# Start offsets for some 150 tasks and a five-transfer queue rule in the list scheduler of an attention and MLP kernel

## The chip, the cores and the metric

The kernel runs on one core of a Trainium2 chip. The metric is the device time of one execution in microseconds (us); lower is better. A core has five instruction streams that run side by side and wait for each other through semaphores: TensorE (PE: matmuls and transposes; its weight loads are shown as PEld), VectorE (DVE), ScalarE (ACT), GpSimd (POOL) and SyncE (SP, which issues all the DMA transfers here). Each stream is strictly in order: an instruction that waits holds back everything behind it on its engine.

## What is computed

Two attentions over the same q, k and v are added, and the sum goes through a two-layer MLP:

```python
# q, k, v: (8 batches, 8 heads, 576 positions, 64)
q_d = q.reshape(B, H, 144, 4, 64).mean(axis=3)        # k_d, v_d alike
out_up = np.repeat(sm_attn(q_d, k_d, v_d), 4, axis=2) # pooled attention, full softmax
mask = np.abs(pos[:, None] - pos[None, :]) < 4        # local attention: 7 neighbours
out_local = softmax(where(mask, q @ k.T * scale, -1e9)) @ v
x = (out_up + out_local).transpose(0, 2, 1, 3).reshape(4608, 512)
h = x @ w_in                                          # 512 -> 2048
return np.maximum(0.01 * h, h) @ w_out                # 2048 -> 512
```

## The kernel before

**Chunks and passes.** The 4,608 rows of x are cut into 13 chunks of columns (batch 0 is chunks 0 and 1 with 256 and 320 columns; chunk 2 has 256, chunk 3 has 320, the rest 384). TensorE makes a pass over the weights for each chunk: for each of 16 slices f of the hidden layer an up-projection into a bank `hp` (`up_proj`, L872), a leaky ReLU on ACT and DVE (`leaky`, L882 to L885), and a down-projection into four banks `acc0` to `acc3`, one for each slice e of the output (`down_proj`, L912). Each product is three matmuls, of a high and a low part of weights and of x, so 24 matmuls for one f. Chunk 0 is done in two passes (f 0 to 7, then, after the pass of chunk 1, f 8 to 15). At the end of a pass `store` copies each `acc` on ACT to a buffer `o` (L957; two buffers in the first pass), and `send` writes it out by DMA. Until the copy is done the bank can't take the next pass.

**Weights.** `convert(f, k)` loads one slice of `w_in` (k=0) or `w_out` (k=1), 512 KB of raw 64-bit numbers, into a staging buffer, and makes the two parts of it with a cast on ACT (L330), a merge on DVE (L332), a second cast on ACT or DVE (L346, L343) and a subtraction on POOL (L348). The first slices stage in buffers that the attention uses later (`k`, `v`, `prod`, `up`); once the work of batch 0 is done, its pool of tiles is given back (`swap`), and the last slices stage in tiles named `w` that lie there.

**Attention.** For batch 0 everything is on TensorE (`pooled`, L451 to L490, and `banded`, L626 to L694). For batches 1 to 7 the pooled part is `pair` (L503 to L581), and the local part runs on POOL and DVE: `scores` (products on POOL at L735, sums on DVE at L743, softmax) and `values` (products on POOL at L794, sums on DVE at L801 into `xloc`). `landing` then turns `xloc` over on TensorE (L831), adds the pooled part (DVE L838) and writes the two parts of x (ACT L844, DVE L846). The first up-projection of a pass waits until all landings of its chunk are done.

**What sets the order.** Every piece of work is a task (a Python generator) with a rank. `Order.run` is a list scheduler that runs while the kernel is built: it keeps a clock for each engine, asks each task for its next operation, and emits the one that can start first by its own costs, the lower rank first where two tie. What it emits stands in that order on the engines for good. The ranks come from `od.spawn(rank, ...)`; for instance a conversion has 20 + 2f + k, the up- and down-projections come last with 4999 and 5000. DMA transfers have one clock too, `wire`, the time when all transfers issued so far would be through at 270 GB/s; a transfer may not be issued while `wire` lies more than 6 us ahead:

```python
if size:
    start = max(start, self.wire - 6.0)
...
if size:
    self.wire = max(self.wire, start + 1.2) + size / RATE
    done = self.wire + 0.8
```

These clocks exist only while the order is made. The chip sees the order and the semaphores, and SP issues a transfer as soon as its buffers are free.

Of the kernel before, what the change touches and what calls it, by code (L numbers as in the profile page):

```python
# [79 lines left out]
OMAX = max(XMAX)  # L80
COST = {"ACT": (0.13, 0.00083), "DVE": (0.08, 0.00104), "POOL": (0.25, 0.00217)}
HOP = 0.4
RATE = 270e3
SAFE = 0.4
POLICIES = [0]
SCARCE, HURRY = ("pt",), 1000
GIVE = {"POOL": 0.3, "DVE": 0.3, "ACT": 0.3}

# [27 lines left out]
class Slot:  # L116
    def __init__(self, order, tag, index, t, task):
        self.order, self.tag, self.index, self.t, self.task = order, tag, index, t, task
        self.push = HURRY if tag in SCARCE else 0
        task[0] -= self.push  # L120
# [6 lines left out]
class Order:  # L127
# [7 lines left out]
    def __init__(self, bufs, policy):  # L135
        self.policy = policy
        self.bufs = bufs
        self.released = {tag: [] for tag in bufs}
        self.engine = dict.fromkeys(("PE", "DVE", "ACT", "POOL", "SP"), 0.0)
        self.wire = 0.0  # L140
        self.port = {"DVE": 0.0, "POOL": 0.0}
        self.events = {}
        self.tasks = []
        self.count = 0
        self.log = []

    def spawn(self, rank, gen):
        self.count += 1
        task = [rank, self.count, gen, None]
        self.tasks.append(task)  # L150
        self.resume(task, None)

# [28 lines left out]
    def run(self):  # L181
        while self.tasks:
            for task in sorted((t for t in self.tasks if t[3][0] != "op"), key=lambda t: t[:2]):
                got = self.grant(task)
                if got is not None:
                    self.resume(task, got)
                    break
            else:
                best = None
                ahead = {eng: [] for eng in GIVE}  # L190
                for task in self.tasks:
                    if task[3][0] == "op" and task[3][1] in GIVE:
                        ahead[task[3][1]].append((max(self.engine[task[3][1]], task[3][3]), task[0]))
                for task in self.tasks:
                    if task[3][0] == "op":
                        _, eng, dur, ready, size, port = task[3]
                        start = max(self.engine[eng], ready)
                        if port:
                            start = max(start, self.port["DVE" if eng == "POOL" else "POOL"])
                        if size:  # L200
                            start = max(start, self.wire - 6.0)
                        if eng in GIVE:
                            late = start + GIVE[eng] * dur
                            start = min((at + 0.01 for at, rank in ahead[eng] if rank < task[0] and start < at < late), default=start)
                        key = (start, task[0], task[1])
                        if best is None or key < best[0]:
                            best = key, task
                assert best is not None, [t[3] for t in self.tasks]
                (start, _, _), task = best
                _, eng, dur, ready, size, port = task[3]  # L210
                free = self.engine[eng]
                self.engine[eng] = start + dur
                if port:
                    self.port[eng] = start + dur
                if size:
                    self.wire = max(self.wire, start + 1.2) + size / RATE
                    done = self.wire + 0.8
                else:
                    done = start + dur + HOP
                self.log.append((start, eng, dur, task[0], start - free, ()))  # L220
                self.resume(task, done)
# [849 lines left out]
```

## Time and profile before

| | |
|---|---|
| median of 3 runs (range) | 934.78 us (931.5 to 936.12) |
| the profiled execution | 935.61 us |
| its span, first to last instruction | 933.8 us |
| mean granted TensorE clock | 0.984 of full speed |
| busy: PE, DVE, ACT, POOL | 910.1, 579.5, 419.8, 568.1 us |
| DMA, mean over the span | 127 GB/s |

The profiled execution lies 0.83 us above the median, and its span 1.81 us below its time, so a span of this kernel and the median differ by 0.98 us. Busy time is that of instructions that ran; idle time of an engine is put down to whatever released it. The granted clock is the share of full speed (2.4 GHz) that TensorE was given, and 0.50 is its other level (1.2 GHz).

### The profile page before, as it was taken

The numbers are of one execution on the slowest core, as the hardware profiler recorded it, in microseconds if no ns is written. First come the engines' busy times: TensorE is split into PE (matmuls) and PEld (weight loads), VectorE is DVE, ScalarE is ACT, GpSimd is POOL, SyncE is SP. The second block draws the span as 40 slices with busy tenths as digits, with TensorE's granted clock in tenths as the row PEclk, the third lists the DMA queues.
The fourth block names the chain that finished last, engine by engine and source line by source line (L and its number), as shares of the span: only waits on it lengthen the run. The fifth ranks groups of instructions, "written<-read, shape, count | busy, mean of one in ns | idle before, by whom it ended". The sixth has DMA issues, their size and how long they took to land.

```text
span 933.8 us, 16676 instructions
## 1 busy us (share of the span) xinstructions
PE 910.1 (97%) x6352; PEld 884.1 (95%) x6352; DVE 579.5 (62%) x941; ACT 419.8 (45%) x1161; POOL 568.1 (61%) x276
## 2 busy tenths in 40 slices
PE   6997999999999999999999999999999999999998
PEld 4787999899999999999999999999999999999998
DVE  4796678878887987876655963953764743311111
ACT  3776547546655545446224544443423423322211
POOL 4555679788889889876966853963974963000000
PEclk7799899999999999999999999999999999999999
DMA  9769565665555554661423541630430410000000
GB/s 243 269 197 315 192 194 153 197 195 145 164 170 162 159 156 113 206 188 56 137 82 106 178 143 29 199 98 26 136 112 26 138 43 26 35 1 1 34 1 35
DMA packets 60977, 118.13 MB, mean 127 GB/s; under 512 B 7440, under 2 KB 26640, under 8 KB 60896
## 3 DMA queue, kind: packets, MB, share of 16 engines
q1 hardware_dynamic: 60896, 117.06, 41.7%
q8 instruction: 50, 0.82, 0.4%
q14 instruction: 31, 0.25, 0.1%
HBM read 107.07 MB, written 9.96 MB: 125 GB/s over the span
## 4 chain that ended last, share of the span: by engine, by line
PE 93%; DVE 2%; DMA 2%; ACT 1%; issue 1%; POOL 1%; SPq 0%; DVEq 0%; POOLq 0%; ACTq 0%
PE acc L912 42%; PE hp L872 42%; PE pt L831 1%; PE pt L533 1%; PE pt L557 1%; PE pt L574 1%; PE acc L451 1%; PE pt L634 1%; DMA w<-in_w_out_dram 1%; DMA vs<-in_vs_dram 1%; POOL w L348 1%; DMA band_sb<-in_band_dram 0%; PE pt L675 0%; PE hp L457 0%; ACT pds L472 0%
## 5 line engine op out<-in xcount | busy, mean ns | idle before, releaser
L794 POOL TENSOR_TENSOR prod<-v,s 128x1344 f32<-128x1344 f32 (+1 forms) x88 | 262.4, 2985 | 84.0 <-DVE xloc L801 78.6
L735 POOL TENSOR_TENSOR prod<-q,k 128x1365 f32<-128x1365 f32 (+1 forms) x88 | 240.1, 2731 | 32.8 <-DVE s L743 20.9
L885 DVE TENSOR_TENSOR gl<-hp,gh 128x384 fp32r<-128x384 f32 (+2 forms) x208 | 108.8, 524 | 243.0 <-ACT hp L883 242.0
L882 ACT ACTIVATE gh<-hp 128x384 fp32r<-128x384 f32 (+2 forms) x208 | 97.5, 469 | 323.6 <-PE acc L912 314.8
L912 PE MATMUL acc<-gh,w 128*128 128x384 f32 (+2 forms) x832 | 217.0, 327 | 0.0
L872 PE MATMUL hp<-xh,w 128*128 128x384 f32 (+2 forms) x832 | 215.9, 327 | 0.6 <-DVE gl L885 0.6
L872 PEld LDWEIGHTS hp<-xh,w 128*128 128x128 f32 x832 | 148.1, 188 | 2.0 <-issue 1.2
L912 PEld LDWEIGHTS acc<-gh,w 128*128 128x128 f32 x832 | 148.3, 188 | 1.3 <-issue 1.0
L912 PE MATMUL acc<-gh,woh 128*128 128x384 f32 (+2 forms) x416 | 138.3, 332 | 5.6 <-ACT o L957 5.5
L872 PE MATMUL hp<-xh,wih 128*128 128x384 f32 (+2 forms) x416 | 140.0, 337 | 0.5 <-DVE gl L885 0.5
L912 PE MATMUL acc<-gh,wol 128*128 128x384 f32 (+2 forms) x416 | 135.7, 326 | 0.5 <-POOL wol L348 0.5
L743 DVE TENSOR_REDUCE s<-prod 128x21 f32<-128x1365 f32 (+1 forms) x88 | 131.4, 1494 | 7.4 <-POOL prod L735 7.3
L912 PE MATMUL acc<-gl,woh 128*128 128x384 f32 (+2 forms) x416 | 135.5, 326 | 0.0
L872 PE MATMUL hp<-xh,wil 128*128 128x384 f32 (+2 forms) x416 | 135.2, 325 | 0.0
L872 PE MATMUL hp<-xl,wih 128*128 128x384 f32 (+2 forms) x416 | 135.2, 325 | 0.0
L912 PE MATMUL acc<-gl,w 128*128 128x384 f32 (+2 forms) x416 | 134.7, 324 | 0.0
L872 PE MATMUL hp<-xl,w 128*128 128x384 f32 (+2 forms) x416 | 134.7, 324 | 0.0
L801 DVE TENSOR_REDUCE xloc<-prod 128x192 f32<-128x1344 f32 (+1 forms) x88 | 130.4, 1481 | 5.3 <-POOL prod L794 5.2
L883 ACT ACTIVATE hp<-hp 128x384 f32<-128x384 f32 (+2 forms) x208 | 96.2, 462 | 0.0
L912 PEld LDWEIGHTS acc<-gh,woh 128*128 128x128 f32 x416 | 78.8, 189 | 8.0 <-ACT o L957 6.0
L872 PEld LDWEIGHTS hp<-xh,wih 128*128 128x128 f32 x416 | 78.5, 189 | 3.2 <-issue 2.0
L912 PEld LDWEIGHTS acc<-gh,wol 128*128 128x128 f32 x416 | 78.7, 189 | 0.7 <-POOL wol L348 0.7
(174 smaller groups left out, 1195.8 us busy)
## 6 DMA issues: line engine op xcount, KB each, us to landing
k<-in_kb_dram SPq DMA_DIRECT2D x76, 292.5 KB, 2.8
v<-in_vb_dram SPq DMA_DIRECT2D x76, 288.0 KB, 2.9
qk<-in_qkt_dram SPq DMA_DIRECT2D x32, 576.0 KB, 7.7
vs<-in_vs_dram SPq DMA_DIRECT2D x56, 144.0 KB, 3.4
q<-in_qb_dram SPq DMA_DIRECT2D x76, 97.5 KB, 1.9
out_dram<-head SPq DMA_DIRECT2D x18, 192.0 KB
out_dram<-o SPq DMA_DIRECT2D x18, 192.0 KB, 2.6
k<-in_kb_dram SPq DMA_DIRECT2D x12, 260.0 KB, 7.6
```

The source lines that it names most:

```text
L348: nc.gpsimd.tensor_tensor(out=lo, in0=tf, in1=hi.bitcast(F32), op=ALU.subtract)
L451: nc.tensor.matmul(sc[rows, qi * SD:(qi + 1) * SD], qk_d[rows, qi * QB:qi * QB + 64], qk_d[rows, SD:2 * SD], start=True, stop=True)
L533: nc.tensor.matmul(scs[p][outs, qi * SD:(qi + 1) * SD], qk_d[i][rows, qi * QB:qi * QB + 64], qk_d[i][rows, SD:2 * SD], start=True, stop=True)
L735: nc.gpsimd.tensor_tensor(out=prv, in0=q[:, :nj].unsqueeze(2).to_broadcast([128, nj, W, DE]), in1=view(half(s_k), 0, [[DE, nj], [DE, W], [ ...
L743: nc.vector.tensor_reduce(out=s[:, p, :nj], in_=prv, axis=AX.X, op=ALU.add)
L794: nc.gpsimd.tensor_tensor(out=prv, in0=view(half(s_v), 0, [[1, nj], [nv, D], [1, W]]), in1=s[:, p, :nj].unsqueeze(2).to_broadcast([128, nj ...
L801: nc.vector.tensor_reduce(out=xl_t[:, :nj, p], in_=prv, axis=AX.X, op=ALU.add)
L872: nc.tensor.matmul(hp[:, :n], wt[:, c], x[:, c], start=k == 0, stop=k == 3 * NC - 1)
L882: nc.scalar.activation(out=gh[:, :n], in_=hp[:, :n], func=AF.Prelu, alpha=0.01)
L883: nc.scalar.activation(out=hp[:, :n], in_=hp[:, :n], func=AF.Prelu, alpha=0.01)
L885: nc.vector.tensor_tensor(out=gl[:, :n], in0=hp[:, :n], in1=gh[:, :n].bitcast(F32), op=ALU.subtract)
L912: nc.tensor.matmul(acc[:, :n], wt[:, es], g[:, :n], start=f == f0 and j == 0, stop=f == f1 - 1 and j == 2)
```

## The change

No operation is added or left out. The scheduler is given another rule for DMA and a table of offsets, and emits another order:

- Instead of the 6 us limit, an operation of SP may not start before the fifth last transfer has landed by the scheduler's clocks (`DEEP = 5`).
- `POLICIES` holds one table, `SHIFTS`, of some 150 numbers by the running number of a task (24 to 224), which `spawn` adds to the task's rank. Most are under 10 in size. They fall on conversions, `pair`, `scores`, `widen` and `values` of the first batches, and on others that are spawned early.

```diff
+DEEP = 5
 RATE = 270e3
 SAFE = 0.4
-POLICIES = [0]
+SHIFTS = {
+    24: 9.7, 27: 5.4, 28: -0.3, 30: 3, 32: 2.8, 33: -0.92, 36: -0.3, 37: -0.52, 38: 1.15, 40: 1.7, 41: 0.95, 42: 8.2, 43: -11.2, 48: -0.3,
...
+}
+POLICIES = [SHIFTS]
...
         self.wire = 0.0
+        self.landed = []
...
-        task = [rank, self.count, gen, None]
+        task = [rank + self.policy.get(self.count, 0), self.count, gen, None]
...
-                        if size:
-                            start = max(start, self.wire - 6.0)
+                        if len(self.landed) >= DEEP and eng == "SP":
+                            start = max(start, self.landed[-DEEP])
...
                     self.wire = max(self.wire, start + 1.2) + size / RATE
+                    self.landed.append(self.wire)
```

All lines behind the table stand 15 lines lower in the changed kernel (L957 is L972 there).

**SP, from the last of the six loads into the given-back tiles.** `w` rows are loads of weights, `up` too; `out_dram<-o` are the first pass's results; `k`, `q`, `vs` and `v` are the first loads for batch 1. Before:

```order
L259 DMA w_0_1013<-in_w_in_dram 128x2048
L259 DMA up<-in_w_out_dram 128x2048
L259 DMA vs<-in_vs_dram 48x768 x2
L259 DMA k<-in_kb_dram 128x520
L259 DMA q<-in_qb_dram 128x130
L259 DMA k<-in_kb_dram 128x520
L259 DMA w_1_1135<-in_w_out_dram 128x2048
L259 DMA out_dram<-o 128x256 x2
```

With the change:

```order
L274 DMA w_0_1039<-in_w_in_dram 128x2048
L274 DMA out_dram<-o 128x256 x2
L274 DMA up<-in_w_out_dram 128x2048
L274 DMA k<-in_kb_dram 128x520
L274 DMA vs<-in_vs_dram 48x768 x2
L274 DMA v<-in_vb_dram 128x512
L274 DMA out_dram<-o 128x256 x2
L274 DMA w_1_1159<-in_w_out_dram 128x2048
```

The first two results go out straight behind the six loads, and the other two ahead of the next load of weights; the six loads stand in one row in both.

**ACT, around the copies of the first pass's results to `o`.** `head<-` rows are the casts of freshly landed weights, `gh` and `hp` rows the leaky ReLU, `acc_693` and `acc_700` (`acc_660` and `acc_666` with the change) the third and the fourth bank. Before, from the copies of the first two banks:

```order
L957 COPY o<-acc_688 128x256
L330 CAST head_76<-w_1_1010 128x512
L882 ACTIVATE gh<-hp 128x320
L883 ACTIVATE hp<-hp 128x320
L346 CAST w_0_1168<-w_0_1009 128x512
L330 CAST head_75<-w_0_1011 128x512
L330 CAST head_76<-w_1_1012 128x512
L346 CAST w_0_1219<-w_0_1011 128x512
L330 CAST head_75<-w_0_1013 128x512
L330 CAST head_76<-w_1_1135 128x512
L957 COPY o<-acc_693 128x256
L957 COPY o<-acc_700 128x256
```

With the change, up to the same copies (those of the first two banks stand five rows ahead of this piece):

```order
L345 CAST head_76<-w_1_1034 128x512
L575 COPY ptd<-pt 128x3x2x48
L897 ACTIVATE gh<-hp 128x320
L898 ACTIVATE hp<-hp 128x320
L345 CAST head_75<-w_0_1035 128x512
L596 COPY outd<-pt 64x144 x4
L897 ACTIVATE gh<-hp 128x320
L898 ACTIVATE hp<-hp 128x320
L972 COPY o<-acc_660 128x256
L972 COPY o<-acc_666 128x256
```

Before, the casts of all six loads and of one load issued after them (`w_1_1135`) stand ahead of the copies of the third and fourth bank; with the change only those of the first two of the six.

**ACT, in the start, from the first cast of weights on.** `pds` is the softmax of heads 4 and 5 (c=2 in `pooled`, with `acc3_229` before and `pt_220` with the change), `su_pd` with `acc0` that of c=3, `su_ptd` and `outd` copies of c=1 to 3, `k_73` and `v_74` the first two loads of weights. Before:

```order
L330 CAST head0_75<-k_73 128x512
L692 CAST xh0_88<-hp_257 128x256
L490 COPY su_ptd_246<-acc1_247 72x3x2x48
L490 COPY su_ptd_246<-pt_297 72x3x2x48
L472 ACTIVATE pds_65,acc3_229<-acc3_229,st_d_255 128x144 x3
L645 ACTIVATE xloc_288<-xloc_288 128x280
L346 CAST wih_0_69<-k_73 128x512
L442 COPY outd_86<-pt_303 128x144
L472 ACTIVATE su_pd_317,acc0_294<-acc0_294,st_d_316 128x144 x3
```

With the change:

```order
L487 ACTIVATE pds_65,pt_220<-pt_220,st_d_242 128x144 x3
L345 CAST head0_75<-k_73 128x512
L707 CAST xh0_88<-acc1_255 128x256
L505 COPY su_ptd_262<-acc2_263 72x3x2x48
L345 CAST head1_76<-v_74 128x512
L505 COPY su_ptd_262<-acc3_315 72x3x2x48
L660 ACTIVATE xloc_291<-xloc_291 128x280
L505 COPY su_ptd_317<-hp_318 72x3x2x48
L505 COPY su_ptd_317<-pt_335 72x3x2x48
L664 ACTIVATE lst_292<-lst_292 128x4
L457 COPY outd_86<-pt_325 128x144
L487 ACTIVATE su_pd_308,acc0_280<-acc0_280,st_d_307 128x144 x3
```

The softmax of c=2 moved ahead of the first cast of weights, the second cast of weights moved up between the copies of c=1, and the softmax of c=3 moved a few places back.

## Rows read from the trace of the kernel before

**Rows 1.** Page, part 1: busy us, share of the span, instructions.
```profile
PE 910.1 (97%) x6352; PEld 884.1 (95%) x6352; DVE 579.5 (62%) x941; ACT 419.8 (45%) x1161; POOL 568.1 (61%) x276
```

**Rows 2.** PE's waits, whole span: us in total, times, longest.
```profile
PE pt L626 <- DMA band_sb<-in_band_dram: 6.1, 1, 6.1
PE acc L912 <- ACT o L957: 5.5, 2, 5.3
...
PE acc L912 <- DVE head L949: 0.2, 1, 0.2
```

**Rows 3.** Windows of the start: length, busy us by engine, PEclk, DMA share, GB/s.
```profile
14.00:26.00 12.00, 12.00 (x87) 8.44 (x85) 5.27 (x14) 5.98 (x21) 5.68 (x7) 0.50 1.02 279
26.00:34.00 8.00, 6.22 (x89) 4.69 (x85) 7.38 (x20) 7.39 (x27) 3.69 (x4) 0.93 0.94 294
34.00:42.00 8.00, 7.65 (x77) 5.71 (x75) 5.20 (x13) 5.54 (x13) 5.33 (x6) 0.50 0.52 172
```

**Rows 4.** Timeline of the start: start, us, instruction, idle before and its releaser.
```profile
23.35 0.77 ACT L330 CAST head<-k 128x512 f16<-128x512 bf16 x1 [1.76 <-DMA k<-in_w_in_dram]
28.03 0.91 POOL L422 TENSOR_TENSOR pds<-pds,st_d 128x432 f32<-128x432 f32 x1 [6.38 <-ACT outd L442]
31.20 0.52 PE L661 MATMUL pt<-id_sb,xloc 128*70 128x128 f32 x3 [1.44 <-DVE xloc L642]
```

**Rows 5.** Chain that ended last, from 84 us: start, us, what.
```profile
84.05 5.24 DMA w<-in_w_out_dram
...
90.00 2.20 DVE w L332
...
92.79 1.40 ACT head L330 x2
94.18 0.23 ACT o L957
...
99.91 3.52 PE hp L872 x24
```

**Rows 6.** Timeline of SP's issues and one DVE sum, same columns as Rows 4.
```profile
72.60 0.33 SPq L259 DMA_DIRECT2D w<-in_w_out_dram  x1
78.39 0.91 SPq L259 DMA_DIRECT2D vs<-in_vs_dram  x2
89.13 0.95 DVE L520 TENSOR_REDUCE v_d<-vs 128x192 f32<-128x768 f32 x1 [2.06 <-DMA vs<-in_vs_dram]
```

**Rows 7.** Windows around PE's long wait, columns as in Rows 3.
```profile
70.00:89.20 19.20, 18.00 (x160) 16.59 (x158) 10.81 (x21) 15.13 (x35) 10.03 (x9) 1.00 0.95 306
89.20:94.50 5.30, 0.04 (x1) 0.04 (x1) 4.60 (x4) 2.27 (x5) 3.98 (x4) 0.70 0.99 360
94.50:98.10 3.60, 3.60 (x14) 3.60 (x15) 0.83 (x3) 0.95 (x3) 1.67 (x1) 0.50 0.97 347
```

**Rows 8.** Timeline of the last landings of chunks 3 and 4, columns as in Rows 4.
```profile
216.63 1.07 DVE L801 TENSOR_REDUCE xloc<-prod 128x128 f32<-128x896 f32 x1
218.91 0.38 PE L831 MATMUL pt<-id_sb,xloc 128*128 128x128 f32 x2
...
281.09 0.55 DVE L846 TENSOR_TENSOR xl<-pt,xh 128x384 fp32r<-128x384 f32 x1
283.05 0.42 PE L872 MATMUL hp<-xh,wih 128*128 128x384 f32 x1
```

**Rows 9.** Window from the long wait to chunk 3, columns as in Rows 3.
```profile
95.00:214.70 119.70, 118.11 (x1016) 114.82 (x1015) 95.36 (x177) 68.99 (x211) 92.47 (x51) 0.99 0.58 180
```

**Rows 10.** POOL's waits, 95 to 140 us, columns as in Rows 2.
```profile
POOL w L348 <- DVE w L343: 7.3, 4, 2.6
POOL w L348 <- ACT w L346: 4.9, 3, 3.6
```

**Rows 11.** ACT's waits, 95 to 140 us, columns as in Rows 2.
```profile
ACT gh L882 <- PE acc L912: 10.0, 9, 2.9
```

**Rows 12.** SP's own waits, whole span, columns as in Rows 2.
```profile
SPq L259 <- ACT o L957: 15.4, 15, 3.6
```

9 rows, old and new, of the table SHIFTS are left out of this document.

## The prediction

> **What bounds the kernel now.** I read the page's busy times first: TensorE is busy 97% of the span [rows 1], so 933.8 - 910.1 = 23.7 us is all the idle time there is, and the change adds and removes no work. A new order can win from two things only: this idle time, and stretches in which TensorE ran at half its clock. So the next view is TensorE's waits [rows 2]. Two of the 14 carry half of the idle time: 6.1 us at the start, for the first data, and 5.3 us for a copy from a bank to `o`. The rest are under 2 us each. Then the windows: from 14 to 26 us and from 34 to 42 us the granted clock was 0.50 [rows 3], and again from 94.5 to 98.1 us, behind the long wait [rows 7]. From there to the end TensorE hardly waits. So the start (to 42 us) and the stretch around 90 us hold what can be won.
>
> **The long wait.** The chain shows what ended it [rows 5]: a load of weights issued at 84.05 landed 5.24 us later, DVE merged it (2.20 us with another), ACT made two casts (1.40 us), and only then came the copy to `o` that frees the bank. The copy itself needed none of this. It stood behind those casts on ACT, which is in order; TensorE was done with the bank long before. DVE had been late too: it held still 2.06 us for a `vs` transfer that was issued at 78.39 and had landed only at 89.13, 10.7 us later [rows 6], because six loads of 512 KB stood in the queue from 72.60 on, with DMA 95 to 99% busy [rows 6, 7].
>
> **The change, part by part.** Base: the profiled span, 933.8 us; the median of the runs is 0.98 us above it.
>
> *The rule of five transfers.* On the chip it costs nothing and limits nothing: it only moves the scheduler's clocks, and SP still has the six loads in one row. What it can do is make the scheduler expect late landings, and place work accordingly.
>
> *The copies on ACT.* They now stand ahead of the casts that held them. What is late next is their target: `o` has two buffers, so the third copy waits until the first result has left, and that transfer now stands right behind the six loads. Six loads and two results are 6 x 0.524 + 2 x 0.131 = 3.41 MB; at the 306 GB/s measured there [rows 7] that is 11.1 us from the first load on, at the 360 GB/s of the next stretch 9.5 us, plus 0.23 us of the copy that the chain shows [rows 5]. Meanwhile TensorE has, by the new order, 12 matmuls of 256 columns and 42 of 320 before it needs that bank. 24 matmuls of 320 columns take 3.52 us, so 0.147 us each [rows 5], and in proportion 0.118 us for 256 columns (an estimate): 6.2 + 1.4 = 7.6 us, and beside them some transposes and products of `pair` that I leave uncosted. So the wait that is left lies between 0 and 11.3 - 7.6 = 3.7 us. I take 1.3, about a third of the bound, since the `pair` pieces and the slower first matmuls lie in between. Gain 5.3 - 1.3 = **4.0 us**, bounds 1.6 and 5.3.
>
> *Half clock behind the long wait.* 14 matmuls took 3.60 us, 0.257 each [rows 7], against 0.147: 14 x 0.110 = 1.5 us. If the wait that is left is short, the clock may not fall; in the start it did fall after waits of 1.78 us in all [rows 3]. I take half, **0.8 us**, bounds 0 and 1.5.
>
> *The start.* ACT waited 1.76 us for the first weights with the softmax of c=2 behind it, and POOL stood 6.38 us until ACT was through [rows 4]; TensorE idled 8.00 - 6.22 = 1.78 us from 26 to 34 us [rows 3], most of it for `xloc` [rows 4]. The new order takes the softmax of c=2 out from behind the cast. In exchange the second cast of weights now stands ahead of the second copy of c=1 and of the softmax of c=3. If that load comes as late as the first one did, it costs 1.76 us again. I take the idle time as won, **1.8 us**. Bounds: -1.8 (the new wait alone), and 1.8 + 3.8 = 5.6, if the half clock from 34 to 42 us goes too: 7.65 us busy at 0.50 [rows 3] would take 3.8 us at full clock. I leave that out, since from 14 to 26 us TensorE was busy 12.00 of 12.00 us and still stood at 0.50 [rows 3]: being busy does not bring the clock back at once.
>
> The Trainium skill (TensorE: Matmul & The Clock Gate, Part 1) says that "the default state is throttled, and activity releases the throttle". By that sentence a start without idle time keeps its clock once it has risen, and the sum would be 3.8 us lower. The 12 us at 0.50 with TensorE busy throughout speak against it, the 0.93 that followed them for it.
>
> *Other short waits.* The new order has its own; I cost them like the old ones, 0. All of them beside the 6.1 and 5.3 us make 12.3 us, of which 1.78 are taken above, and part is the kernel's end, where the last results leave. I take a quarter of them, 3 us, as bounds either way (an estimate).
>
> *Whether the gain survives the next passes.* TensorE can start the pass of a chunk only when its x is written, and before the change the passes of chunks 3 and 4 start just behind that: the last x of chunk 4 was written at 281.64 and its pass began at 283.05 [rows 8]. If TensorE is 6.6 us early, x must be early as well. For the last piece of chunk 3, `xloc` was ready at 217.70 and TensorE turned it over at 218.91 [rows 8]: only 1.2 us of slack. The rest must come from POOL and DVE. POOL was busy 92.47 of 119.70 us from 95 us to there [rows 9], 27.2 us idle, and 12.2 us of waits in it were for casts of weights on DVE and ACT [rows 10], which stand behind the leaky ReLU there; ACT spent 10.0 us waiting for TensorE's matmuls [rows 11]. So much of the lateness of x is TensorE's own, and goes when TensorE is early. I take **0.8 us** of loss, bounds 0 and 5.4 (all of the 6.6 but the slack of 1.2).
>
> Sum: 4.0 + 0.8 + 1.8 - 0.8 = 5.8 us. 933.8 - 5.8 = 928.0 us of span, and with 0.98 a median of **929.0 us**, 0.6% less.
>
> **The rivals.**
>
> *The clock stays up in the start.* For it: a start without the idle time from 26 to 34 us; against it: the row from 14 to 26 us. 929.0 - 3.8 = 925.2 us. The sentence quoted above from the Trainium skill would have it so.
>
> *Attention sets the pace.* x of chunk 3 comes no earlier than its slack lets it, so that TensorE waits at the start of its pass and gives back all but 1.2 us: 934.8 - 1.2 = 933.6 us. For it: POOL and DVE have no slack left at chunk 3 [rows 8], and the new order has every down-projection before chunk 2 done when its pass starts, where the old one had one f left to fill in with. Against it: the waits in [rows 10, 11].
>
> *The change doesn't do what it says.* The chip knows no limit of five, the six loads still stand in a row, and the wait of 5.3 us only changes its name. Then the start alone counts: 934.8 - 1.8 = 933.0 us.
>
> *Slower: SP holds the attention's loads.* SP is in order, and now waits for copies of results before it may issue `up`, `k`, `vs` and `v`, and again for the second pair before `w`, `v`, `q` and `k`. In the old order the first loads of `scores` were issued ahead of the results. SP's waits for these copies were 3.6 us at most [rows 12]. The second pair can be copied only when the first has left, about 11.3 us behind the first load, at some 72.6 + 11.3 = 83.9 us by the old clock [rows 6]; a second hold of 3.6 us at the results of the next pass would add up, and 1.5 us of half clock after the waits that follow. If all of it reaches x: 3.6 + 3.6 + 1.5 = 8.7 us on top of a start that loses 1.8 us instead of winning it: 934.8 + 8.7 = 943.5 us, or up to 945.3 us. The point from which this decides can be read off: the work behind the last x of chunk 4 is the same but for one f of down-projection that is done earlier (12 x 0.147 = 1.8 us), so the kernel is slower than before if that x comes later than 281.64 + 1.8 = 283.4 us, and by over 0.5% if it comes after 288 us.
>
> **How the numbers follow.** A difference of 0.5% (4.7 us: under 930.1 or over 939.5 us) is about what a measurement of this kernel can tell from no change. My forecast, 929.0 us, gets 0.44; the clock that stays up 0.16; attention setting the pace 0.20; the wait that stays 0.09; the held loads 0.11. Faster: 0.44 + 0.16 = 0.60; same: 0.20 + 0.09 = 0.29; slower: 0.11. The forecast lies 1.1 us inside its own class. Range: downwards to the clock's 925.2 less 3 us of short waits and the 0.7 us of clock that I halved, 921.5 us; upwards to the 933.6 us of the pace plus 3 us of short waits, 936.6 us. That leaves out the held loads and little else.
>
> **What would show it.** In the profile of the changed kernel: the wait for a copy to `o` under 2 us and no window at half clock behind it (else the term of 4.0 + 0.8 is wrong); no wait for `xloc` around 30 us, and the first up-projection before 41 us; the granted clock from 34 to 42 us (0.50, or the rival); the last x of chunk 3 near 216 us and of chunk 4 near 276 us. If TensorE instead waits at the start of the passes of chunks 2 to 4, the pace was the limit. If SP waits for copies of results longer than 3.6 us and the first `scores` starts late on POOL, it is the held loads. I would be wrong altogether if TensorE's total of busy time changes by more than some 3 us at the same clock, for then the order itself costs matmul time.

## The result and the profile after the change

| | before | after |
|---|---|---|
| median of the runs | 935.45 us (931.5 to 937.88, 4 runs) | 924.64 us (924.1 to 926.19, 4 runs) |
| ratio to before, 95% interval | | 0.9891 [0.9854, 0.9928] |
| the profiled execution, its span | 935.61, 933.8 us | 926.19, 924.3 us |
| mean granted TensorE clock | 0.984 | 0.991 |

The changed kernel is 1.1% faster. Its median, 924.64 us, lies 4.4 us under the forecast of 929.0 and inside the range of 921.5 to 936.6 us; the span is 9.5 us shorter, where 5.8 us were predicted.

The two mean clocks in the table are no evidence of a difference. The profile's record of the clock begins only at 9.4 us before and at 20.9 us after, and what lies ahead of it is counted as 1.00, while the matmuls there ran at half speed (for the changed kernel shown below). With 0.50 put there, both means are 0.98 (an estimate from these figures).

The first view is again the page's busy times; TensorE's idle time is 924.3 - 907.4 = 16.9 us, where it was 23.7 [rows 1]:

```profile
PE 907.4 (98%) x6352; PEld 881.9 (95%) x6352; DVE 583.7 (63%) x941; ACT 419.0 (45%) x1161; POOL 570.2 (62%) x276
```

The waits of TensorE over the whole span (us in total, times, longest). The 5.3 us for a copy to `o` [rows 2] are 0.7 us now; the first row, for the first data, is nearly as it was (5.7 us for 6.1). The wait for `su_ptd` is new:

```profile
PE pt L641 <- DMA su_vs<-in_vd_dram: 5.7, 1, 5.7
...
PE pt L472 <- ACT su_ptd L505: 1.0, 1, 1.0
...
PE acc L927 <- ACT o L972: 0.7, 1, 0.7
```

The windows that answer to those around the long wait [rows 7] (length, busy us of PE, PEld, DVE, ACT, POOL, then the granted clock, DMA share, GB/s). TensorE is busy throughout at 1.00. In the 3.60 us in which 14 matmuls of 320 columns ran before, 27 are counted now, of which 24 begin in it, all of 320 columns:

```profile
89.20:94.50 5.30, 5.30 (x39) 5.30 (x38) 4.83 (x8) 4.23 (x8) 4.28 (x3) 1.00 1.05 375
94.50:98.10 3.60, 3.60 (x27) 3.60 (x26) 3.30 (x4) 0.63 (x2) 2.38 (x2) 1.00 1.00 369
```

What the third copy waits for now, in the timelines of SP and ACT (start, us, instruction, idle before and its releaser). The six loads begin at 74.41, the first two results go out at 77.27, and the copy starts at 85.30, 10.9 us behind the first load, once a result has left `o`:

```profile
74.41 0.33 SPq L274 DMA_DIRECT2D w<-in_w_out_dram  x1
...
77.27 0.88 SPq L274 DMA_DIRECT2D out_dram<-o  x2
```

```profile
85.30 0.70 ACT L972 COPY o<-acc 128x256 f32<-128x256 f32 x2 [1.55 <-DMA out_dram<-o]
```

The windows of the start, to be held against [rows 3]:

```profile
14.00:26.00 12.00, 11.22 (x95) 7.52 (x93) 6.92 (x19) 7.20 (x25) 6.54 (x8) 1.00 1.01 284
26.00:34.00 8.00, 7.42 (x82) 5.48 (x84) 7.35 (x16) 6.77 (x24) 4.08 (x4) 0.61 0.82 263
34.00:42.00 8.00, 7.23 (x74) 5.59 (x71) 5.69 (x15) 5.34 (x13) 5.87 (x5) 0.50 0.73 230
```

The 1.00 of the first row holds only from 20.9 us on, where the record of the clock begins. Three transposes of 112 columns show it; the first two rows are of the kernel before (at 0.50, then at 1.00), the other two of the changed one:

```profile
14.62 0.77 PE L488 MATMUL acc<-id_sb,su_pd 112*72 112x112 f32 x3
32.44 0.45 PE L488 MATMUL pt<-id_sb,su_pd 112*72 112x112 f32 x3
14.05 0.77 PE L503 MATMUL acc<-id_sb,su_pd 112*72 112x112 f32 x3
22.23 0.48 PE L503 MATMUL acc<-id_sb,su_pd 112*72 112x112 f32 x3
```

So with the change TensorE had full speed from 20.9 to 27.7 us and half speed around it, to 44.8 us; before, it had full speed from 9.4 to 12.8 and from 26.5 to 33.3 us. That is not the change's doing: the clock of the start differs between executions of one order. pool_late and copies_late (below) have the changed kernel's order on all five streams up to 78 us, and here are the same three transposes in the two:

```profile
30.43 0.77 PE L503 MATMUL hp<-id_sb,su_pd 112*72 112x112 f32 x3
30.37 0.48 PE L505 MATMUL hp<-id_sb,su_pd 112*72 112x112 f32 x3 [0.98 <-POOL su_pd L439]
```

ACT's timeline in the start shows where the new wait for `su_ptd` comes from: the cast of the second weights (`v`) waits for its load, and the second copy of c=1 stands behind it until 25.84:

```profile
25.21 0.77 ACT L345 CAST head<-v 128x512 f16<-128x512 bf16 x1 [0.46 <-DMA v<-in_w_out_dram]
25.84 0.38 ACT L505 COPY su_ptd<-acc 72x288 f32<-72x288 f32 x1
```

The chain of the start (start, us, what) shows what that load holds up: behind the cast and the copy comes, by way of DVE, a product of the softmax on POOL, and TensorE waits for it:

```profile
15.88 9.30 DMA v<-in_w_out_dram
25.18 0.02 issue
25.21 0.77 ACT head L345
25.97 0.26 ACT su_ptd L505
...
29.84 0.92 POOL su_pd L437
30.75 0.04 issue
30.80 0.77 PE hp L503 x3
```

The first up-projection starts where it started before:

```profile
41.19 0.58 PE L872 MATMUL hp<-xh,wih 128*128 128x256 f32 x1
41.19 0.56 PE L887 MATMUL hp<-xh,wih 128*128 128x256 f32 x1
```

The agreement to the hundredth is chance. With the order of the changed kernel it came at 40.33 to 41.19 us (after, copies_late, pool_late, conv_only), with the order of the kernel before at 40.71 to 41.19 (before, copies_first, results_first). So the start gained some 0.2 us on average, and 0.9 us at most. Two rows tell of the pace of the attention: the last x of chunk 4, and the pass that uses it. Before, 1.4 us lay between the two, at 281.64 and 283.05 [rows 8]; now x is ready at 268.57, 9.5 us ahead of its pass:

```profile
268.02 0.55 DVE L861 TENSOR_TENSOR xl<-pt,xh 128x384 fp32r<-128x384 f32 x1
```

```profile
278.11 0.34 PE L887 MATMUL hp<-xh,wih 128*128 128x384 f32 x1
```

And SP's own waits for copies of results, which were 15.4 us with 3.6 the longest [rows 12]:

```profile
SPq L274 <- ACT o L972: 8.9, 15, 1.6
```

### The profile page after: what moved, and what is told of

Read it like the earlier page. It is cut to its first block, busy times and chain, and to the rows that moved or that the text cites. A ratio compares the mean times of both kernels' runs of the same rounds, so it can differ in the third digit from the quotient of the medians.

```text
span 924.3 us, 16673 instructions
## 1 busy us (share of the span) xinstructions
PE 907.4 (98%) x6352; PEld 881.9 (95%) x6352; DVE 583.7 (63%) x941; ACT 419.0 (45%) x1161; POOL 570.2 (62%) x276
## 4 chain that ended last, share of the span: by engine, by line
PE 94%; DMA 3%; DVE 1%; ACT 1%; issue 0%; POOL 0%; SPq 0%; POOLq 0%; ACTq 0%
PE acc L927 44%; PE hp L887 43%; PE pt L846 1%; PE pt L548 1%; PE pt L589 1%; PE pt L572 1%; DMA su_vs<-in_vd_dram 1%; DMA v<-in_w_out_dram 1%; DMA out_dram<-o 1%; PE pt L690 0%; DMA qk<-in_qkt_dram 0%; PE pt L676 0%; ACT head L345 0%; PE pt L649 0%; DVE s L758 0%
## 5 line engine op out<-in xcount | busy, mean ns | idle before, releaser
L750 POOL TENSOR_TENSOR prod<-q,k 128x1365 f32<-128x1365 f32 (+1 forms) x88 | 241.1, 2742 | 23.7 <-DVE s L758 8.2
L758 DVE TENSOR_REDUCE s<-prod 128x21 f32<-128x1365 f32 (+1 forms) x88 | 131.7, 1496 | 10.9 <-POOL prod L750 10.9
L887 PEld LDWEIGHTS hp<-xh,wil 128*128 128x128 f32 x416 | 78.8, 189 | 0.5 <-POOL wil L363 0.5
```

The lines of the kernel that those rows point to most:

```text
L750: nc.gpsimd.tensor_tensor(out=prv, in0=q[:, :nj].unsqueeze(2).to_broadcast([128, nj, W, DE]), in1=view(half(s_k), 0, [[DE, nj], [DE, W], [ ...
L758: nc.vector.tensor_reduce(out=s[:, p, :nj], in_=prv, axis=AX.X, op=ALU.add)
L887: nc.tensor.matmul(hp[:, :n], wt[:, c], x[:, c], start=k == 0, stop=k == 3 * NC - 1)
```

## The experiments

My theory after the result: one bank was held by two things that stand in order, ACT's casts and SP's transfers, and opening both is worth some 7 of the 10 us; the rest is that the attention keeps up with the earlier TensorE. The rivals: the order as a whole carries the gain; any disturbance of the old order helps; the clock in the start counts; the attention's offsets do it.

The table gives all runs. The ratio is to the kernel before on the same chip. The three columns at the right are TensorE's idle time (length of the window less its busy time) in the start, in the stretch with the long wait, and from there to 920 us. They are of one execution each, and the first depends on the clock, since matmuls at full speed leave more of the window idle: for one order of the start (after, copies_late, pool_late, conv_only) it goes from 10.06 to 13.05 us.

| kernel | median us | ratio [95%] | idle 0-42 | 42-95 | 95-920 |
|---|---|---|---|---|---|
| before | 935.45 | 1 | 11.12 | 7.31 | 1.75 |
| after | 924.64 | 0.9891 [0.9854, 0.9928] | 10.06 | 2.26 | 0.99 |
| copies_late | 933.14 | 0.9969 [0.9958, 0.998] | 11.10 | 7.19 | 2.21 |
| copies_first | 936.06 | 0.9997 [0.9985, 1.0008] | 10.61 | 5.75 | 3.76 |
| results_first | 932.12 | 0.997 [0.9949, 0.999] | 10.65 | 1.78 | 4.06 |
| rule_alone | 931.03 | 0.9947 [0.9931, 0.9962] | 11.07 | 4.01 | 2.05 |
| offsets_alone | 925.62 | 0.9887 [0.9871, 0.9904] | 10.35 | 2.97 | 0.99 |
| conv_only | 926.13 | 0.9914 [0.9886, 0.9942] | 13.05 | 2.47 | 1.17 |
| attn_only | 931.47 | 0.996 [0.9943, 0.9978] | 12.62 | 2.01 | 2.93 |
| warm | 926.38 | 0.9909 [0.9875, 0.9943] | 12.55 | 3.44 | 0.99 |
| pool_late | 932.14 | 0.9962 [0.9946, 0.9978] | 11.36 | 2.47 | 4.94 |
| v_back | 935.67 | 1.0003 [0.9986, 1.002] | 9.30 | 2.68 | 6.55 |
| jitter | 928.2 | 0.9922 [0.9892, 0.9951] | 12.41 | 2.28 | 2.80 |
| shuffled | 943.04 | 1.0081 [1.0051, 1.0111] | 16.71 | 3.43 | 4.42 |

### The copies put back behind the casts

On the changed kernel, in `convert` and `store`:

```diff
         t = yield from op("ACT", 790, t, s_u.t)
+        if (f, k) == (12, 1):
+            od.signal("cast")
...
                 s_o, o = yield from place(p)
+                if p == 0 and e > 1:
+                    yield from wait("cast")
```

> The changed kernel with one thing undone: in the first pass, the copies of the third and fourth bank to the result buffer may be emitted only after ACT's cast of the slice of w_out for f 12, so that on ACT the casts of all six loads and of one later load stand ahead of them, as in the kernel before. The rest of the order is the scheduler's own reaction to that. Theory (the long wait and the half clock behind it carry the gain): a wait for a copy of some 4 to 6 us comes back near 90 us, the clock falls to 0.50 behind it, and the time is 5 to 7 us over the changed kernel's 924.6: 930 to 932 us. Rival (the gain is spread over the whole order, and later waits take up what is won here): the wait comes back but the passes of chunks 2 to 4 start as early as in the changed kernel, 924 to 927 us.

The wait is back, and the half clock behind it. TensorE's row and two windows of this kernel:

```profile
92.58 0.64 PE L929 MATMUL acc<-gh,woh 128*128 128x320 f32 x1 [5.59 <-ACT o L976]
```

```profile
88.00:92.00 4.00, 0.00 (x0) 0.00 (x0) 2.49 (x4) 0.47 (x1) 0.86 (x2) 0.71 1.03 384
92.00:96.50 4.50, 3.92 (x15) 3.92 (x16) 2.14 (x3) 2.83 (x7) 3.91 (x3) 0.50 0.93 326
```

The ratio goes from 0.9891 to 0.9969: of the 1.09% that the change gives, this one place carries 0.78%, or 7.3 us (with both intervals, 3.6 to 11). That is a little over the theory's 5 to 7 us, and the rival is out. In the trace it is 4.9 us more idle time from 42 to 95 us, 1.2 us behind that, and the half clock. On SP the first two results still leave straight behind the six loads, at 75.68 us, so it is ACT's order that is tested here.

### The same place done on the kernel before

First only ACT's order, then SP's as well:

```diff
+        if n >= 5:
+            yield from wait("first", 4)
         t = yield from op("ACT", 790, t, s_u.t)
...
+            if p == 0:
+                od.signal("first")
             if c1 == n:
```

> The kernel before, without the new rule and without offsets, with one thing done: ACT's casts of the late loads from the third of the six on may be emitted only when all four copies of the first pass have been emitted. So the third and fourth copy stand ahead of those casts, as with the change; the results' transfers still stand behind the first loads of batch 1 on SP, so the copies come somewhat later than with the change. Theory: the wait of 5.3 us shrinks to 1 to 3 us and the time is 3 to 6 us under before's 935.4: 929 to 932 us, without any table of offsets. Rival (the rest of the order made the gain, above all that x of chunks 3 and 4 comes early enough to use it): the passes of chunks 3 and 4 then wait for x and the time stays within 2 us of before, 933 to 937 us.

No gain, 0.9997, where the theory had 3 to 6 us. The copies stand ahead of the casts on ACT, and still start at 92.19 us, since `o` was not empty: the result in it was issued only at 86.62, behind the first loads of batch 1 and two more loads of weights. ACT's and SP's rows:

```profile
92.19 0.70 ACT L959 COPY o<-acc 128x256 f32<-128x256 f32 x2 [5.39 <-DMA out_dram<-o]
```

```profile
86.62 2.08 SPq L259 DMA_DIRECT2D out_dram<-o  x2
```

So the wait has a second lock. It did shrink, from 5.3 to 3.8 us, but TensorE then idled 3.76 us behind 95 us, 2.0 us more than before. The next kernel is copies_first with this one too (in `run`, besides the signals that count the six loads and the results):

```diff
+                        if size and self.events.get("six", (0,))[0] == 6 and self.events.get("sent", (0,))[0] < 2 and task[2].__name__ != "send":
+                            continue
                         start = max(self.engine[eng], ready)
```

> The kernel before (old limit of 6 us, no offsets) with two things done: as in copies_first, ACT's casts from the third late load on stand behind the four copies of the first pass; and once the six loads are issued, SP may issue nothing but the first two results, so that they stand right behind the six loads as with the change. In copies_first the copies had moved, but the buffer for the third one was empty only at 92.19 us, since the result in it left late. Theory (the wait has two locks, ACT's order and SP's order, and the change opens both): the wait for the copy falls under 1.5 us, the clock stays at 1.00 behind it, and PE begins the second half of chunk 0 at about 137 us instead of 140.5. If x keeps up, 928 to 931 us. Rival (the attention sets the pace): SP now holds the first loads of batch 1 until the copies of the first pass at about 83 us are done, x of chunks 2 and 3 comes no earlier than before (170.2 and 222.1 us), and the time stays at 933 to 937 us with waits at those passes.

Both locks open, the wait for a copy is 0.3 us, and the idle time up to 95 us is 12.43 us, as with the change (12.32). But the time gains only 0.30%, 2.8 us: behind 95 us TensorE idles 4.06 us where it idled 1.75. The longest of these waits, in TensorE's timeline and in DVE's just ahead of it:

```profile
149.43 0.39 PE L878 MATMUL hp<-xh,w 128*128 128x256 f32 x1 [1.51 <-DVE gl L891]
```

```profile
147.16 1.55 DVE L749 TENSOR_REDUCE s<-prod 128x21 f32<-128x1365 f32 x1
148.62 0.42 DVE L852 TENSOR_TENSOR xl<-pt,xh 128x256 fp32r<-128x256 f32 x1
148.95 0.42 DVE L891 TENSOR_TENSOR gl<-hp,gh 128x256 fp32r<-128x256 f32 x1
```

The leaky ReLU (`gl`) stands behind a sum and a landing of the attention, and TensorE waits for it. So theory and rival are each half right: the wait goes as said, and the attention then takes back 2.3 us as idle time, not at the start of a pass, but through DVE's order.

One thing keeps this kernel from being the change without its table. The first results were copied only at 82.71 us (76.07 with the change), and SP, which might issue nothing else, stood 6.8 us for them with the first loads of batch 1 behind (SP's waits, 74 to 98 us):

```profile
SPq L261 <- ACT o L963: 6.8, 1, 6.8
```

Those loads went out 5 to 7 us later than before (`vs` at 85.56 for 78.39). Whether the attention was late for that or for want of its offsets is not shown.

### What delays in the attention cost

To measure that by itself, the changed kernel with one product of POOL made four times:

```diff
-            nc.gpsimd.tensor_tensor(
+            for _ in range(4 if (b, j0, u, p) == (1, 0, 0, 0) else 1):
+                nc.gpsimd.tensor_tensor(
```

> The changed kernel with POOL's first product of values (128x896, 2.1 us, near 118 us) made four times over instead of once, into the same place; the three additional ones serve nothing and add 6.3 us to POOL, unknown to the scheduler. POOL is idle for some 13 us from 95 to 140 us and for about 7 from 166 to 214 us with the change. Theory (x has next to no slack at chunks 2 and 3, so a later attention stops TensorE): x of chunk 2 comes 3 to 6 us later than 166.5 us, TensorE waits for it, and the time is 3 to 6 us over 924.6: 927.5 to 930.5 us. Rival (POOL's idle time and the down-projections that TensorE has in hand take it up): x of chunk 3 is back at 215 to 217 us and the time within 1.5 us of 924.6.

The four products take 8.70 us where one took 2.13, so 6.6 us were added, and the ratio rises by 0.71%, 6.6 us (with both intervals, 2.9 to 10.4). That is over the theory's 3 to 6 us, and the rival, which had 1.5 at most, is out. The rows of POOL, of DVE's sum that waits for the product, and of TensorE:

```profile
117.24 8.70 POOL L810 TENSOR_TENSOR prod<-v,s 128x896 f32<-128x896 f32 x4
```

```profile
125.98 1.09 DVE L817 TENSOR_REDUCE xloc<-prod 128x128 f32<-128x896 f32 x1 [6.34 <-POOL prod L810]
```

```profile
131.12 0.41 PE L888 MATMUL hp<-xh,w 128*128 128x320 f32 x1 [3.95 <-DVE gl L901]
```

The path is another than the theory's: DVE, in order, stands 6.34 us before its sum, a merge and a leaky ReLU stand behind that, and TensorE stops 3.95 us at 127 us, long before the pass of chunk 2. The granted clock was 0.74 from 130 to 134 us. Behind 95 us TensorE idles 3.95 us more than with the change, and the profiled execution is 5.2 us longer; so most of the delay went through, but whether all of it did is not shown.

### The start

In the changed kernel, the second cast of weights moved behind both copies of c=1:

```diff
+        if (f, k) == (0, 1):
+            yield from wait("turned", 2)
         t = yield from op("ACT", 790, t, s_u.t)
...
+            if c == 1:
+                od.signal("turned")
         s_pd.free(tt)
```

> The changed kernel with one more condition: ACT's first cast of the second load of weights (v, w_out of f 0) may be emitted only when both copies of c=1 in pooled have been emitted. In the changed kernel this cast waited for its load until 25.18 us with the second copy behind it, and TensorE waited 1.0 us for that copy; the clock fell to 0.50 soon after. The scheduler then also orders the copies of the first pass a little otherwise (two late casts stand between the second and the third copy, and the first results stand behind four loads on SP). Theory (this wait costs the start): the first up-projection starts 1 to 3 us before 41.19. For the time: 922 to 925 us if the place of the results still lets the third copy come by 88 us; 927 to 931 us if the results leave as late as with the rule alone.

The start is won and the rest lost. The first up-projection comes at 39.13 us, 2.1 us earlier than with the change and 1.0 us earlier than in any other run here. So the second cast is what held the start up, as far as a start can show it whose other operations the scheduler placed anew. The wait for a copy to `o` is 0.5 us, and the time is that of before, 1.0003. From 166 to 215 us TensorE idles 4.75 us (0.78 with the change), and the clock falls with it. Two rows of TensorE, and two windows:

```profile
167.36 0.66 PE L850 MATMUL pt<-id_sb,xloc 128*128 128x128 f32 x2 [2.36 <-DVE st_p L498]
...
171.33 0.79 PE L576 MATMUL pt<-id_sb,pds 112*128 112x112 f32 x3 [2.02 <-DVE s L774]
```

```profile
166.00:170.00 4.00, 1.94 (x8) 1.68 (x8) 3.93 (x9) 3.00 (x12) 2.77 (x2) 0.64 0.67 204
170.00:174.00 4.00, 2.67 (x13) 2.71 (x14) 3.95 (x7) 2.42 (x7) 3.52 (x3) 0.50 0.35 96
```

DVE is busy all the time (3.93 and 3.95 of 4.00 us) with the attention, and TensorE waits for it at a landing and at a piece of `pair`. From 166 to 178 us 43 matmuls run at a clock of 0.57; with the change it is 111 at 1.00. Neither of my two cases for the time foresaw it; both went by the place of the results, which was harmless here. It was the prediction's rival that the attention sets the pace, in full. Since the condition also shifted the whole plan behind it, this run shows that a faster start can be lost at 166 us, not that it must be.

The other run on the start, matmuls in front of TensorE's short waits, in three places like this one:

```diff
+        if (b, c) == (0, 1):
+            for _ in range(4):
+                nc.tensor.matmul(sc[:, :128], id_sb, id_sb, start=True, stop=True)
         dots(sc, qk_d)
```

> The changed kernel with 15 additional matmuls of 128 columns whose results nobody reads: 6 ahead of the scores of c=1 in banded, 4 ahead of its dots and 5 ahead of its mixed product in pooled, each into a bank that the real matmul then overwrites. They stand in front of TensorE's short waits before 30 us, to see whether the fall of the clock to 0.50 from 28 to 44 us costs time. Theory that the clock is what the start loses: the clock stays at 1.00 there and the first up-projection starts 2 to 5 us earlier, 920 to 923 us. Theory that the weights set the pace (from f 3 on the first pass starts each up-projection 0.05 to 1.2 us behind the moment when its weights are ready): the first up-projection may start earlier, but the time stays within 1.5 us of 924.6. If the added matmuls only lengthen the start: 925 to 927 us.

```profile
26.00:34.00 8.00, 5.76 (x100) 4.29 (x94) 7.93 (x17) 6.61 (x23) 4.33 (x5) 1.00 0.80 258
34.00:42.00 8.00, 6.26 (x56) 5.10 (x57) 6.04 (x14) 5.30 (x14) 5.61 (x5) 0.57 0.78 275
```

```profile
84.53 0.73 ACT L981 COPY o<-acc 128x256 f32<-128x256 f32 x2 [2.73 <-DMA out_dram<-o]
```

TensorE had full speed from 10.4 to 34.3 us, 24 us where the changed kernel had 7, and the first up-projection came at 40.12 us, 1.1 us earlier than there and 0.2 us earlier than the best of the other runs of this start. So the clock is not what the start loses. The time is the same within its interval (0.9909 against 0.9891), where the third case, that the added matmuls only lengthen the start, had put it. The six loads were issued 2.0 us earlier too, but the result behind them left only 0.8 us earlier (84.5 for 85.3), so TensorE waited 1.8 us for the copy instead of 0.7, and this time the clock fell: two matmuls of 320 columns behind the wait, and two later ones, begin 0.27 and 0.15 us apart:

```profile
87.11 0.47 PE L896 MATMUL hp<-xh,wih 128*128 128x320 f32 x1
87.38 0.47 PE L896 MATMUL hp<-xl,wih 128*128 128x320 f32 x1
...
90.11 0.31 PE L896 MATMUL hp<-xh,wih 128*128 128x320 f32 x1
90.26 0.31 PE L896 MATMUL hp<-xl,wih 128*128 128x320 f32 x1
```

What the start gained ended at the queue of transfers. That the weights set the pace, as I had it, is not what the trace shows.

### Which part of the change

```diff
-POLICIES = [SHIFTS]
+POLICIES = [{}]
```

> The changed kernel with an empty table: the rule of five transfers alone. On ACT the casts of three late loads stand between the second and the fourth copy (six and one more before, none with the change), and the first results stand behind four small loads on SP. Theory (copies are what counts): the long wait is about halved, and the time lies between the two kernels, 928 to 933 us. Rival (the rule does nothing by itself, the table does all): within 2 us of before, 933 to 937 us. A rule that works alone would give 924 to 926 us.

```diff
-                        if len(self.landed) >= DEEP and eng == "SP":
-                            start = max(start, self.landed[-DEEP])
+                        if size:
+                            start = max(start, self.wire - 6.0)
```

> The changed kernel with the old limit of 6 us on the queue in place of the rule of five transfers, and the whole table of offsets. Two late casts stand ahead of the last two copies, as with the change, and the first results stand right behind the six loads; the second pair of results stands behind more loads. Theory (the place of the copies counts): most of the gain, 924 to 928 us, with the wait for the third copy under 2 us. Rival (offsets that were searched for one rule fit only that rule): 930 to 937 us, with waits for x at the passes of chunks 3 to 5.

The rule alone gives half the gain (0.53%), through the same place: its waits for copies to `o` are 2.4 us. The table alone gives all of it (0.9887 and 0.9891 are the same), so on top of it the rule adds nothing that can be measured. The next two split the table at key 79; conv_only is shown, shortened; attn_only keeps what this one drops and drops the rest:

```diff
     52: -0.33, 55: 0.3, 57: 0.3, 60: 0.5, 61: -0.3, 66: 0.3, 69: -0.9, 70: -0.9, 71: -0.54, 72: 0.3, 74: 0.3,
-    79: 0.6, 80: -10, 83: -1.2,
...
```

> The changed kernel with the offsets of the attention of batches 1 to 7 taken out (keys from 79 on); the offsets of batch 0 and of the conversions and the rule of five stay. The start and the stretch around 85 us should be as with the change. Theory (the offsets of batch 0 and of the conversions make the gain, since these set where the copies and results stand): 924 to 927 us. Rival (without its own offsets the attention is late, and sets the pace at chunks 2 and 3): x of chunk 3 near 218 us instead of 214.4, TensorE waits there, 927 to 932 us.

> The changed kernel with only the offsets of the attention of batches 1 to 7 (keys from 79 on); those of batch 0 and of the conversions are taken out. ACT's casts of three late loads then stand between the second and the fourth copy, as with the rule alone. Theory: the same as the rule alone, 929 to 932 us, with a wait for a copy of about 2 us. Rival (the attention's offsets carry the gain): 924 to 927 us, with the passes of chunks 3 and 4 starting near 215 and 278 us all the same.

The 25 offsets of batch 0 and of the conversions carry the gain. The 103 of the attention, by far the most of the table, do no more by themselves than the rule does without any, and left out they cost at most a little (0.9914, the intervals overlap). In attn_only the wait for copies was down to 1.1 us and the idle time from 42 to 95 us as short as with the change, and still the gain is 0.40%: it idles 2.93 us behind 95 us, and its first up-projection comes at 41.47. Like results_first and v_back it shows that the open place is needed but not enough.

Last, two tables of the same size of numbers:

```diff
-    24: 9.7, 27: 5.4, 28: -0.3, 30: 3, 32: 2.8, 33: -0.92, 36: -0.3, 37: -0.52, 38: 1.15, 40: 1.7, 41: 0.95, 42: 8.2, 43: -11.2, 48: -0.3,
+    24: 8.2, 27: -0.3, 28: 1.15, 30: 0.95, 32: -0.92, 33: 9.7, 36: 1.7, 37: -0.52, 38: -0.3, 40: 5.4, 41: 2.8, 42: 3, 43: 0.3, 48: -0.54,
...
```

> The changed kernel with the numbers of the table dealt out anew at random, each within its own kind of task (batch 0, conversions, attention of batches 1 to 7). Theory (the gain hangs on where few transfers and copies stand, which the search found): such a table is worth nothing, 930 to 940 us. Rival (any disturbance of the old order helps): 924 to 929 us.

```diff
-    24: 9.7, 27: 5.4, 28: -0.3, 30: 3, 32: 2.8, 33: -0.92, 36: -0.3, 37: -0.52, 38: 1.15, 40: 1.7, 41: 0.95, 42: 8.2, 43: -11.2, 48: -0.3,
+    24: 9.46, 27: 6.32, 28: -0.64, 30: 2.02, 32: 1.89, 33: -1.58, 36: 0.27, 37: -0.79, 38: 0.73, 40: 0.89, 41: 1.91, 42: 8.05, 43: -11.78, 48: -1.18,
...
```

> The changed kernel with every offset moved at random by up to 1 either way. In this order two late casts stand between the second and the third copy on ACT as with the change, but the first results stand behind four loads on SP. Theory (the place of the results on SP is the second lock): a wait for a copy of 1 to 4 us comes back near 88 us, 927 to 931 us. Rival (the table as a whole carries the gain, small moves do not matter): 924 to 926.5 us.

Dealt out at random the table makes the kernel 0.8% slower than before, 943.04 us, where the theory had 940 at most: the first up-projection starts at 61.38 us. That any disturbance helps is out, as far as one draw can tell. Moved by up to 1, it keeps 0.78% of the 1.09%. The time (928.2 us) is the one that the theory gave, but not for its reason: the wait did not come back, though the first results left at 83.84 us behind five loads (0.7 us in all for copies to `o`). It idles 1.8 us more behind 95 us; its 2.3 us more in the start are no loss, as the first up-projection comes at 40.44. The first results were copied only at 83.44, so SP's place held them back by nothing. The place of the results on SP is not always the lock, only where a full bank comes early enough to need it.

## Why the prediction was right, and where not

**The bound and the place** were right: idle time and half clock, with the one long wait worth most. copies_late shows it directly.

**The long wait**, taken as 4.0 us: 4.8 (5.5 to 0.7 us in the waits). The mechanism is the one described, down to the next thing late: the result that has to leave `o`, estimated at 11.1 us behind the first load, measured 10.9. TensorE came to the bank 10.65 us behind the first load, not 7.6: the 54 matmuls were as counted, and the rest is 33 small ones of `pair`, which were left uncosted, and 0.7 us of other idle time. That the wait came out near the 1.3 us taken is a third of a bound hitting well, not a calculation.

**Half clock behind it**, taken as 0.8: all of the bound, 14 x (0.257 - 0.147) = 1.5 us; in the same 3.60 us, 24 matmuls of this size begin with the change, 0.15 us each. Halving it was wrong: the short wait before it (0.7 us) did not bring the clock down.

**The start**, taken as 1.8: 0 in this pair of profiles, at most 0.9 over the runs of the two orders. This is the step that failed. The wait for `xloc` went, but the price of the second cast, which the prediction named at 1.76 us as a bound and then put at nothing, had to be paid: the load came late, TensorE waited 1.0 us for the copy behind it, POOL's product came late in turn, and v_back, which takes this cast out of the way, starts the first up-projection 1.2 to 2.1 us earlier than the runs with the cast in its place. I also took idle time of TensorE as time won, and it is not: the start's idle time fell by 1.1 us and the matmuls of batch 0 took 1.3 us longer (38.9 for 37.6 us over their lines), since in this execution TensorE had 6.8 us of full speed ahead of the first up-projection, and 10.2 us before. Over the runs idle time in the start and its end have little to do with each other: 13.05 us idle with conv_only and the first up-projection at 40.84, 10.06 idle with the change and 41.19.

**Other short waits and the next passes**, taken as 0 and -0.8: the idle time from 95 us on fell by 0.8 instead. The last x of chunk 4 came 13 us earlier, far below the deciding 283.4 us. This was the luckiest term. results_first, pool_late and v_back show that the loss is real (2.3 us of idle time, and 6.6 and some 10 us of time) when the attention is late; the bounds of 0 to 5.4 were sensible, the value held for this order alone.

**The sum.** 5.05 (idle time from 42 to 95 us) + 1.5 + 0.8 = 7.35 of the 9.5 us. The other 2 lie in the matmuls of the up- and down-projections, whose busy time fell by 3.6 us (821.1 to 817.5, summed over their lines), 1.5 of it behind the long wait. Where the rest of that sits was not traced, and stays open; executions of the kernel before differ by more (931.5 to 937.88 us). The total was forecast too low by the halved clock and the loss that didn't come, and the start's 1.8 us, which didn't come either, hid part of that: that is luck.

**The rivals.** The clock that stays up in the start gave nearly the measured time, 925.2 us, and is wrong all the same: from 34 to 42 us it was 0.50, and warm, where the clock did stay up to 34 us, gained 1.1 us at most in the start and no time. The sentence quoted from the Trainium skill (TensorE: Matmul & The Clock Gate, Part 1), that activity releases the throttle, is not borne out there as an immediate thing: TensorE was busy 7.23 of 8.00 us at 0.50. Attention setting the pace did not happen in this kernel, and does in its neighbours. The held loads did not come: SP's waits for copies got shorter; in results_first they did, with 6.8 us. That the wait only changes its name is what copies_first does, so it was a sound rival for half of the change.

## What to carry to other kernels

Where an engine stands still for a copy, look for everything that stands in order ahead of that copy and of what empties its target: opening one lock of two gave nothing here. Price a wait together with the half clock behind it, and count time won on one engine only when the engine that feeds it next is shown to be early as well. Idle time ahead of a fixed point (here the first up-projection) is no gain until that point moves. Check a granted clock against the pace of equal matmuls before reading anything from it.

## What the runs showed of the hardware

Two executions with one order on all streams up to there can have different clocks in the same place: at 30.4 us three equal transposes took 0.77 us in pool_late and 0.48 us in copies_late, and the first up-projection came at 40.80 and 40.33. TensorE ran at half clock for 13 us while busy nearly throughout (before, 12.8 to 26.4 us: 13.41 of 13.60 us). In these rows the busy time of TensorE tells neither the work done nor the clock: from 26 to 34 us it was busy 5.76 of 8.00 us with 100 matmuls at 1.00 (warm), and 7.42 us with 82 at 0.61 (after). Behind six loads of 512 KB a result of 128 KB was out 10.9 to 12.1 us after the first of them was issued (after and conv_only 10.9, offsets_alone 11.4, warm 12.1), and in warm issuing the loads 2.0 us earlier brought it out only 0.8 us earlier.
